# Attention, top-k and expert layer on one core: the first three head pairs get their own order of steps, PSUM banks and copy engines

## The chip, the cores and the metric

One of the eight cores of a Trainium2 chip runs the whole program. The metric is the device time of one execution in microseconds.

## The reference

Eight batches of eight heads, 576 tokens, 64 numbers a head. Attention is masked by blocks of 64 tokens: a token sees its own block and the blocks before it.

```python
scores = scale * np.matmul(q, k.transpose(0, 1, 3, 2))          # (8, 8, 576, 576)
scores = np.where(block_i >= block_j, scores, -1000000000.0)
scores = scores - np.max(scores, axis=-1, keepdims=True)
attn = np.exp(scores)
attn = attn / (np.sum(attn, axis=-1, keepdims=True) + 1e-09)
x = np.matmul(attn, v)                                          # then (8, 576, 512)
# for each batch b
scores = x[b] @ w_gate                                          # (576,)
top_idx = np.argpartition(-scores, 128)[:128]
xe = x[b, top_idx]
out[b] = x[b]
out[b, top_idx] += sigmoid(scores[top_idx])[:, None] * (np.maximum(xe @ w1, 0) @ w2)
```

## The kernel before

**Pairs and tiles.** Two heads form a pair, so there are 32 pairs, 0 to 31. A pair's scores are cut into nine tiles, t = 0 to 8: tile t is the 64 tokens of block t against the 64 (t + 1) tokens that they see, with one head in each half of the 128 partitions. So tile t is 128 x 64 (t + 1), and a shape names its tile: 320 columns are tile 4, 512 tile 7, 576 tile 8.

**The steps of a pair.** `scores(p, u)` (L374) multiplies q and k on TensorE in three parts: u = 2 writes tiles 4, 3, 0 and 2, u = 1 tiles 6, 5 and 1, u = 0 tiles 8 and 7. `maxima(p, t)` (L383) reduces a tile out of PSUM on VectorE. `exps(p, t)` (L393) takes the exponential out of PSUM into `p_sb` on ScalarE, with the maximum as bias. `turn_p(p, w)` (L438) transposes blocks of `p_sb` on TensorE into PSUM, for tile pairs (8, 7), (6, 5), (2, 1), (4, 3) and the halves "h": 16, 12, 4, 8 and 6 transposes, 46 in all. `keep_p` copies them to SBUF, on ScalarE (L217) or VectorE (L224). `times_h` (L488) and `times_v` (L500) multiply with V. `invert` and `divide` (L511, L512, L519) normalise on VectorE, and SP stores the result. `shrink` (L321) scales q on POOL (on VectorE for pair 0, L319).

**The order.** The engines work off their instructions in the order in which the program issues them, and a table sets that order: `STEPS` gives each step a time within a pair, pair p's step is due at p plus that time, and the steps of all pairs are sorted by it. The loop takes the first step that is `ready`: its inputs are issued, the pair before has issued the same step, and the PSUM banks that the step opens are free. `OVER` can give the first pairs times of their own; before, it is empty.

**PSUM.** It has eight banks of 512 columns. `BANK` names the banks of each use: ("s", g) for the score tiles, in five groups (`SETS`: 6 and 8, 7, 4 and 0, 5 and 1, 3 and 2), ("t", u) for the three groups of turns, "y" for the products with V. Odd pairs use them with 2, 3 and 4, 5 exchanged (`OTHER`). So pair 0's turns of group 1 need banks 0 and 1, which hold pair 1's tiles 5, 1 and 7 once pair 1's scores are issued.

**Fillers.** `WAKES` puts matmuls without a use (L743, 512 columns) into waits: eight at time 0.25 and six at 1.3, behind the ten at the very start.

**The rest.** Each pair's output is stored, each batch's gate scores go through ranks and indices (VectorE, POOL, `select`), and behind the attention the selected rows go through w1 and w2 (L953, L977).

Of the kernel before, what the change touches and what calls it, by code (L numbers as in the profile page):

```python
# [103 lines left out]
STORE, FETCH = 0.7, 1.4  # L104
PRELOAD = {"load": 3, "load_v": 2}
WARM, SOON, NQK, FILLS, EARLIEST, BEGIN = 10, 1, 3, 1, 4, 0.3
OVER = {}
FIRST_CUTS = ((0, 320), (320, 576))
FIRST_WRITES = {2: [(2, 0), (4, 2), (2, 4), (4, 3)]}
ENGINE_FIRST = {}  # L110
WAKES = ((0.25, 8), (1.3, 6))
HELD = (6, 7)
WIDE, SHORT, TAGS = (1, 2, 3, 0), (4, 5), {(0, 3): 'w'}
LAST_RANK, LAST_VEC, LAST_FAR = 0.2, 9, 9
# [40 lines left out]
def attention_topk_ffn(  # L155
# [75 lines left out]
    def attention(att):  # L231
# [6 lines left out]
        st = [dict() for _ in range(N)]  # L238
# [4 lines left out]

        def bank(p, use):

            return tuple(OTHER[x] for x in BANK[use]) if p % 2 else BANK[use]

        def take(p, use, reads):

            x = bank(p, use)  # L250
            for z, y in enumerate(x):
                assert live[y] is None, (p, use, live)
                live[y] = [p, use, reads[z] if isinstance(reads, list) else reads]
            return ps_all[:, x[0]:x[-1] + 1:max(x[-1] - x[0], 1), :]

        def give(p, use, part=None):
            for x in bank(p, use)[slice(None) if part is None else slice(part, part + 1)]:
                assert live[x][0:2] == [p, use], (p, use, live)
                live[x][2] -= 1
                if not live[x][2]:  # L260
                    live[x] = None

        now = [0.0]
        uses = {
            "scores": lambda u: [("s", g) for g, _ in WRITES[u]],
            "turn_p": lambda w: [("t", TURNS[w][0])], "times_h": lambda: ["y"],
            "rank": lambda: ["rk"],
        }
        takes, seen = [[] for _ in range(8)], set()
        for at, name, *args in STEPS:  # L270
            for use in uses.get(name, lambda *x: [])(*args):
                if use not in seen:
                    seen.add(use)
                    for p in range(2):
                        for x in bank(p, use):
                            takes[x].append(at + p)

        def room(x):
# [137 lines left out]
        def engine(p, *key):  # L416

            return ENGINE_FIRST.get((p, *key)) or ENGINE[key if len(key) > 1 else key[0]]

# [266 lines left out]
        def tick(kind, p):  # L686
# [15 lines left out]
            turn_p=turn_p, keep_p=keep_p, times_v=times_v, divide=divide,  # L702
# [28 lines left out]
        for p in range(N + 5):  # L731
            for i, (at, name, *args) in enumerate(STEPS):
                if name in TICKS:
                    plan += [(at + x, i, x, name, args) for x in (range(9) if not p else (p + 8,))]
                elif name not in PRELOAD or p >= PRELOAD[name]:
                    plan.append((p + (OVER.get(p, OVER.get(p - N, {})) if p < N else {}).get((name, *args), at), i, p, name, args))
        plan += [(at, -1, 0, "wake", (n,)) for at, n in WAKES]
        plan.sort()
# [23 lines left out]
        firsts = {}  # L762
# [4 lines left out]
        def ready(p, name, args):  # L767

            if p and (p - 1, name, *args) not in made and not (name in PRELOAD and p <= PRELOAD[name]):
                return False  # L770
            for other, back in needs.get(name, ()):
                if p >= back and any((p - back, other, *x) not in made for x in by_name[other]):
                    return False
            return all(
                live[x] is None
                for use in uses.get(name, lambda *x: [])(*args) if firsts[use] == (name, args) for x in bank(p, use)
            )

        parts, owner, filled, warmed = {}, {}, {}, []
# [37 lines left out]
        while (N - 1, "divide") not in made:  # L817
            blocked = set()
            for n, (at, i, p, name, args) in enumerate(plan):
                if name in TICKS or name == "wake" or p >= N or (p not in blocked and ready(p, name, args)):  # L820
                    break
                blocked.add(p)
            at, i, p, name, args = plan.pop(n)
            now[0] = at
            if name == "wake":
                wake(*args)
                continue
            if name in TICKS:
                if name == "rank" and at > N + LAST_RANK or name == "vec" and at > N + LAST_VEC or name == "far" and at > N + LAST_FAR:
                    continue  # L830
                if name != "rank" or all(live[x] is None for x in bank(p, "rk")):
                    tick(name, p)
                continue
            if p < N:
                steps[name](p, *args)
                made.add((p, name, *args))
                if name == "times_v" and p == N - 1 and fill and not warm and "last" not in parts and not any(parts[x] for x in warmed):
                    parts["last"] = list(hidden_parts(0, fill.pop(0), spare(True)))
            elif early:
                stand_in(p, name, args)  # L840
            if name == "scores" and args[0] == 1 and 2 <= p < N:
                weights(p)
            if not early and all((N - 1, "scores", u) in made for u in range(len(WRITES))):
                begin_early()
# [239 lines left out]
    with ExitStack() as att:  # L1084
        const_att = att.enter_context(tc.tile_pool(name="const_att", bufs=1))
        attention(att)
# [31 lines left out]
```

## Time and profile before

| | us |
|---|---|
| median of 3 runs | 350.02 (347.95 to 350.79) |
| profiled execution | 349.31 |
| its span, first to last instruction | 347.6 |
| TensorE matmuls busy | 333.6 (96%) |
| VectorE busy | 254.1 (73%) |
| ScalarE busy | 237.1 (68%) |
| POOL busy | 169.7 (49%) |

Busy times are those of the profiled execution; its time lies 1.7 us above its span, for what comes before the first and after the last instruction. The attention takes about the first 250 us of the span, the expert phase the rest. The shares are means over both.

### The profile page before, as it was taken

What the parts mean: (1) busy time and instruction counts of PE and PEld (TensorE: products, weight loads), DVE (VectorE), ACT (ScalarE), POOL (GpSimd) and SP (SyncE); (2) the same over time, 40 slices, a digit from 0 to 9 for tenths busy, and PEclk for the clock granted to TensorE, in tenths of its full rate; (3) what the DMA queues carried; (4) which work ended last, traced back from release to release, by engine and by line L of the source; (5) the groups of instructions that cost most, each with busy time, mean ns of one, the idle gap of its engine ahead of it and who ended that gap; (6) DMA issues with size and microseconds to landing.
All of it is one profiled execution on the core that took longest, in us unless ns stands there. A gap on an engine that the chain in (4) does not pass through costs nothing.

```text
span 347.6 us, 15612 instructions
## 1 busy us (share of the span) xinstructions
PE 333.6 (96%) x6681; PEld 278.0 (80%) x6681; DVE 254.1 (73%) x638; ACT 237.1 (68%) x554; POOL 169.7 (49%) x240
## 2 busy tenths in 40 slices
PE   8799999999999999999899999999999979999993
PEld 3488888888888888888688888889877768888882
DVE  4567789789979988988798998898296965222330
ACT  3899999999999899998889899997133101122000
POOL 2200056029980569967175895739539933210121
PEclk9999999999999999999999999999999989999998
DMA  7656677676888678666756767341230102200001
GB/s 263 215 165 197 194 214 256 202 240 175 267 245 259 205 224 248 189 182 169 196 153 214 226 177 204 101 111 36 55 84 1 38 31 62 91 31 2 30 30 60
DMA packets 42069, 52.51 MB, mean 151 GB/s; under 512 B 8680, under 2 KB 30736, under 8 KB 42000
## 3 DMA queue, kind: packets, MB, share of 16 engines
q1 hardware_dynamic: 40432, 47.03, 45.7%
q0 software_dynamic: 1280, 4.20, 3.5%
q8 instruction: 52, 0.85, 1.0%
q10 hardware_dynamic: 288, 0.30, 0.3%
q14 instruction: 17, 0.14, 0.1%
HBM read 39.94 MB, written 11.55 MB: 148 GB/s over the span
## 4 chain that ended last, share of the span: by engine, by line
PE 83%; POOL 5%; DVE 4%; issue 2%; ACT 2%; DMA 2%; POOLq 0%; DVEq 0%
PE ps L374 23%; PE ps L500 22%; PE ps L438 14%; PE ps L977 9%; PE ps L953 8%; PE ps L488 4%; POOL more L615 3%; ACT p_sb L393 2%; PE ps L924 1%; PE ps L743 1%; DMA xe<-out_dram,idx_all 1%; POOL count L615 1%; DVE junk L545 1%; DMA out_dram<-y,idx_all 1%; DVE nmax L383 1%
## 5 line engine op out<-in xcount | busy, mean ns | idle before, releaser
L393 ACT ACTIVATE p_sb<-ps,nmax 128x320 f32<-128x320 f32 (+8 forms) x288 | 130.2, 531 | 14.2 <-DVE nmax L383 7.9
L383 DVE TENSOR_REDUCE nmax<-ps 128x1 f32<-128x320 f32 (+8 forms) x288 | 118.9, 480 | 12.1 <-PE ps L374 11.7
L374 PE MATMUL ps<-qk 64*64 64x64 f32 (+6 forms) x1408 | 87.1, 386 | 2.7 <-issue 2.3
L217 ACT COPY pt<-ps 128x512 f32<-128x512 f32 (+1 forms) x192 | 82.2, 507 | 7.6 <-PE ps L438 6.0
L500 PE MATMUL ps<-v,pt 128*64 128x65 f32 x2560 | 81.3, 222 | 0.0
L500 PEld LDWEIGHTS ps<-v,pt 128*64 128x64 f32 x2560 | 77.9, 137 | 1.9
L374 PEld LDWEIGHTS ps<-qk 64*64 64x64 f32 x1408 | 48.8, 133 | 15.8 <-issue 8.8
L615 POOL TENSOR_SCALAR more<-sB,sc 64x64 int8<-64x64 f32 (+6 forms) x49 | 56.8, 1166 | 6.0 <-DMA xe<-out_dram,idx_all 3.7
L438 PE MATMUL ps<-ident,p_sb 64*128 64x64 f32 x1472 | 54.3, 225 | 2.2 <-ACT p_sb L393 2.2
L438 PEld LDWEIGHTS ps<-ident,p_sb 64*128 64x128 f32 x1472 | 49.3, 139 | 5.7 <-issue 2.0
L977 PE MATMUL ps<-w,h 128*128 128x512 f32 x192 | 47.3, 404 | 0.0
L977 PEld LDWEIGHTS ps<-w,h 128*128 128x128 f32 x192 | 36.8, 194 | 8.3
L953 PE MATMUL ps<-xeTh,w 128*128 128x512 f32 x128 | 41.6, 401 | 0.0
L959 ACT ACTIVATE h<-ps 128x512 fp32r<-128x512 f32 x16 | 9.6, 599 | 38.7 <-PE ps L953 38.7
L332 POOL MEMSET v<- 128x14 f32 x32 | 4.0, 124 | 57.0 <-DMA v<-in_vz_dram 49.2
L488 PEld LDWEIGHTS ps<-v,ph 64*64 64x64 f32 x768 | 22.3, 133 | 11.8 <-issue 11.1
L545 DVE CUSTOM_DVE_ANT_0 junk<-x_sb,wg_b 128x512 bf16<-128x512 f32 x40 | 30.8, 769 | 0.1
L987 POOL DMA_INDIRECT out_dram<-y,idx_all x8 | 8.4, 1051 | 44.9 <-DVE y L982 34.7
L960 DVE SCALAR_TENSOR_TENSOR h<-ps,h 128x512 fp32r<-128x512 f32 x16 | 11.0, 690 | 25.3 <-ACT h L959 25.3
L953 PEld LDWEIGHTS ps<-xeTh,w 128*128 128x128 f32 x128 | 24.1, 188 | 6.0
L519 DVE TENSOR_TENSOR x_sb<-ps,rinv 128x640 f32<-128x640 f32 x32 | 26.4, 825 | 1.3
L321 POOL TENSOR_SCALAR qk<-qk 128x576 f32<-128x576 f32 x31 | 22.2, 716 | 10.3 <-DMA qk<-in_qk_dram 7.7
(56 smaller groups left out, 276.2 us busy)
## 6 DMA issues: line engine op xcount, KB each, us to landing
qk<-in_qk_dram SPq DMA_DIRECT2D x31, 576.0 KB, 5.4
v<-in_v_dram SPq DMA_DIRECT2D x32, 264.0 KB, 5.2
w_raw<-in_w_dram SPq DMA_DIRECT2D x16, 256.0 KB, 2.9
out_dram<-x_sb SPq DMA_DIRECT2D x32, 128.0 KB, 3.8
out_dram<-x_sb SPq DMA_DIRECT2D x64, 64.0 KB, 3.2
v<-in_vz_dram SPq DMA_DIRECT2D x32, 99.0 KB, 4.2
sB<-line SPq DMA_DIRECT2D x8, 192.0 KB, 2.9
out_dram<-x_sb SPq DMA_DIRECT2D x32, 32.0 KB, 3.0
```

What stands on the lines that cost most here:

```text
L217: nc.scalar.copy(out=o, in_=i)
L374: nc.tensor.matmul(place(p, t)[64 * o:64 * o + 64, c0:c1], qT[:, 64 * t:64 * t + 64], kT[:, k0:k0 + c1 - c0], start=True, stop=True,)
L383: nc.vector.tensor_reduce(out=s["nmax"][:, c:c + 1], in_=place(p, t), axis=AX.X, op=ALU.max, negate=True)
L393: nc.scalar.activation(out=st[p]["p"][:, first(t):first(t) + ends(t)], in_=place(p, t), func=AF.Exp, bias=st[p]["nmax"][:, c:c + 1], scale ...
L438: nc.tensor.transpose(out=ps[:, a, at], in_=win, identity=ident[r, r])
L488: nc.tensor.matmul(y[64 * c:64 * c + 64, k:k + D + 1], s["ph"][r, a, w], block, start=(z, c) not in begun, stop=False)
L500: nc.tensor.matmul(y[64 * c:64 * c + 64, k:k + D + 1], s["pt"][:, at:at + 64], vt[:, n, hh, 0:D + 1], start=False, stop=hh == 1 and (i, n) ...
L519: nc.vector.tensor_tensor(out=x[:, :, h * D:(h + 2) * D].rearrange("p i (h d) -> p i h d", h=2), in0=outcome(p)[:, :, :, 0:D], in1=rinvs[p ...
L545: nc.vector.tensor_tensor_reduce(out=junk[:, 0:DM], in0=x[:, PLACES.index(t), :], in1=wg_b, scale=1.0, scalar=0.0, op0=ALU.mult, op1=ALU.a ...
L615: eng.tensor_scalar(out=o[r, c:c1], in0=row["sB"][r, c:c1], scalar1=sc[r, t:t + 1], scalar2=None, op0=op)
L953: nc.tensor.matmul(ps[:, 0:ncol], w1_hl[f][:, a, c, :], xeT[g][d][:, c, 0:ncol], start=(c == 0 and t == 0), stop=(c == NC1 - 1 and t == 2),)
L977: nc.tensor.matmul(ps[0:n, 0:DM], h_tile(f)[:, a, begin[g][gi]:begin[g][gi] + n], late["w2"][f][:, d, :], start=(f == 0 and t == 0), stop= ...
```

## The change

The tables for pairs 0, 1 and 2 get entries: `OVER` (times), `BANK_FIRST` (banks), `ENGINE_FIRST` (copy engines). `WAKES` keeps three matmuls of fourteen. `bank` looks into `BANK_FIRST` first. `takes`, by which a spare bank is chosen, asks for pairs 4 and 5, which have no entries. `ready` asks for the banks of each use that the pair has not opened yet, where it asked only at the step that opens a use first in the common table.

```diff
-OVER = {}
+OVER = {
+    0: {
+        ('scores', 2): -0.5767,
+        ('scores', 0): -0.477,
...
+    1: {
+        ('scores', 2): -0.5402,
...
-ENGINE_FIRST = {}
-WAKES = ((0.25, 8), (1.3, 6))
+ENGINE_FIRST = {
+    (0, 'keep_p', (2, 1)): 'act',
+    (0, 'keep_p', (4, 3), 0): 'dve',
+    (0, 'keep_p', (6, 5), 0): 'dve',
+    (0, 'keep_p', (6, 5), 1): 'dve',
+    (0, 'keep_p', (8, 7), 1): 'dve',
+    (1, 'keep_p', (2, 1)): 'act',
+    (1, 'keep_p', (4, 3), 1): 'dve',
+    (1, 'keep_p', (8, 7), 1): 'dve',
+    (2, 'keep_p', (4, 3), 1): 'dve',
+    (2, 'keep_p', (6, 5), 0): 'dve',
+    (2, 'keep_p', (8, 7), 0): 'dve',
+    (2, 'keep_p', (8, 7), 1): 'dve',
+}
+BANK_FIRST = {
+    (0, ('s', 0)): (3, 4),
+    (0, ('s', 1)): (0,),
+    (0, ('s', 2)): (1,),
...
+    (0, ('t', 0)): (1, 4),
+    (1, ('s', 1)): (3,),
...
+}
+WAKES = ((0.25, 3),)
...
         def bank(p, use):
 
+            if (p, use) in BANK_FIRST:
+                return BANK_FIRST[p, use]
             return tuple(OTHER[x] for x in BANK[use]) if p % 2 else BANK[use]
...
-                        for x in bank(p, use):
+                        for x in bank(p + 4, use):
...
-                for use in uses.get(name, lambda *x: [])(*args) if firsts[use] == (name, args) for x in bank(p, use)
+                for use in uses.get(name, lambda *x: [])(*args) if use not in st[p] for x in bank(p, use)
```

The lines of the new kernel are 136 to 138 higher: L374 becomes L512, L438 L576, L383 L521, L393 L531, L217 L353, L224 L360, L743 L881, L488 L626, L500 L638.

TensorE, before, from the first turns of pair 0 on (qk1 is pair 1's q and k, p_sb_150 holds pair 0's exponentials; the fillers between are left out):

```order
L438 MATMUL ps_93<-ident_71,p_sb_150 128x64 x16
L374 MATMUL ps_93<-qk1_121 64x64 x2
L374 MATMUL ps_93<-qk1_121 64x256 x4
L374 MATMUL ps_93<-qk1_121 64x192 x2
L374 MATMUL ps_93<-qk1_121 64x64 x2
L374 MATMUL ps_93<-qk1_121 64x448 x2
L374 MATMUL ps_93<-qk1_121 64x384 x2
L374 MATMUL ps_93<-qk1_121 64x128 x2
L374 MATMUL ps_93<-qk1_121 64x64 x2
L374 MATMUL ps_93<-qk1_121 64x512 x4
```

and TensorE after, at the same place:

```order
L512 MATMUL ps_93<-qk1_121 64x64 x2
L512 MATMUL ps_93<-qk1_121 64x256 x4
L512 MATMUL ps_93<-qk1_121 64x192 x2
L512 MATMUL ps_93<-qk1_121 64x64 x2
L576 MATMUL ps_93<-ident_71,p_sb_150 128x64 x16
L512 MATMUL ps_93<-qk1_121 64x448 x2
L512 MATMUL ps_93<-qk1_121 64x384 x2
L512 MATMUL ps_93<-qk1_121 64x128 x2
L512 MATMUL ps_93<-qk1_121 64x64 x2
L512 MATMUL ps_93<-qk1_121 64x512 x4
L576 MATMUL ps_93<-ident_71,p_sb_150 128x64 x16
```

Part 2 of pair 1's scores has moved ahead of pair 0's turns (8, 7), and the turns (2, 1) and (6, 5) of pair 0 follow pair 1's scores directly, where six fillers stood. Pair 2's scores are cut in the same way, around the turns "h" and (4, 3) of pair 0 and (8, 7) of pair 1.

ScalarE, before, the first eleven exponentials and copies between (pt takes the turned blocks):

```order
L393 ACTIVATE p_sb<-ps,nmax 128x320
L393 ACTIVATE p_sb<-ps,nmax 128x64
L393 ACTIVATE p_sb<-ps,nmax 128x384
L393 ACTIVATE p_sb<-ps,nmax 128x128
L393 ACTIVATE p_sb<-ps,nmax 128x256
L393 ACTIVATE p_sb<-ps,nmax 128x512
L393 ACTIVATE p_sb<-ps,nmax 128x576
L393 ACTIVATE p_sb<-ps,nmax 128x448
L393 ACTIVATE p_sb<-ps,nmax 128x192
L217 COPY pt<-ps 128x2x4x64 x2
L393 ACTIVATE p_sb<-ps,nmax 128x320
L393 ACTIVATE p_sb<-ps,nmax 128x64
```

and after:

```order
L531 ACTIVATE p_sb<-ps,nmax 128x256
L531 ACTIVATE p_sb<-ps,nmax 128x512
L531 ACTIVATE p_sb<-ps,nmax 128x64
L531 ACTIVATE p_sb<-ps,nmax 128x320
L531 ACTIVATE p_sb<-ps,nmax 128x128
L531 ACTIVATE p_sb<-ps,nmax 128x576
L531 ACTIVATE p_sb<-ps,nmax 128x384
L531 ACTIVATE p_sb<-ps,nmax 128x448
L353 COPY pt<-ps 128x2x4x64
L531 ACTIVATE p_sb<-ps,nmax 128x192
L531 ACTIVATE p_sb<-ps,nmax 128x256
L531 ACTIVATE p_sb<-ps,nmax 128x192
```

Tile 7 (512 columns) is now second, and one of the two copies of the turns (8, 7) has gone to VectorE. The next rows there are pair 1's tiles 0, 4 and 5, the copy of (2, 1), and tiles 7, 1, 8 and 6.

VectorE, before, from the end of pair 0's scaling to the first normalising step:

```order
L319 TENSOR_SCALAR qk_120<-qk_120 128x256
L383 TENSOR_REDUCE nmax<-ps 128x1 x18
L224 COPY pt<-ps 128x2x128
L383 TENSOR_REDUCE nmax<-ps 128x1 x9
L511 TENSOR_SCALAR rinv_115<-ps 128x10
```

and after:

```order
L457 TENSOR_SCALAR qk_120<-qk_120 128x256
L521 TENSOR_REDUCE nmax<-ps 128x1 x13
L360 COPY pt<-ps 128x2x4x64
L521 TENSOR_REDUCE nmax<-ps 128x1 x5
L360 COPY pt<-ps 128x2x3x64 x2
L360 COPY pt<-ps 128x2x2x64
L521 TENSOR_REDUCE nmax<-ps 128x1
L360 COPY pt<-ps 128x2x4x64
L521 TENSOR_REDUCE nmax<-ps 128x1 x8
L649 TENSOR_SCALAR rinv_115<-ps 128x10
```

Five copies, two of 512 columns, two of 384 and one of 256, stand among the maxima of pairs 1 and 2, where one of 256 stood.

## Rows read from the trace of the kernel before

**Rows 1.** Chain that ended last, in order of time: start us, us, what.

```profile
7.47 3.01 ACT p_sb L393 x6
10.61 0.72 PE ps L438 x16
...
14.05 3.00 ACT p_sb L393 x6
...
17.09 1.16 PE ps L438 x30
18.25 2.59 PE ps L374 x34
20.84 0.40 PE ps L488 x21
21.23 2.48 PE ps L500 x80
23.72 1.59 PE ps L438 x46
...
28.30 2.48 PE ps L500 x80
...
170.58 1.68 issue
...
257.58 1.22 POOL xe L910
```

**Rows 2.** Timeline of VectorE, ScalarE and POOL at the start (a line begins with start and length).

```profile
5.65 3.78 DVE L383 TENSOR_REDUCE nmax<-ps 128x1 f32<-128x320 f32 x9 [0.79 <-PE ps L374]
7.10 0.28 DVE L383 TENSOR_REDUCE nmax<-ps 128x1 f32<-128x128 f32 x1
12.33 3.67 DVE L383 TENSOR_REDUCE nmax<-ps 128x1 f32<-128x320 f32 x9 [2.89 <-PE ps L374]
...
6.37 0.73 ACT L393 ACTIVATE p_sb<-ps,nmax 128x320 f32<-128x320 f32 x2 [3.17 <-DVE nmax L383]
7.47 3.31 ACT L393 ACTIVATE p_sb<-ps,nmax 128x384 f32<-128x384 f32 x7 [0.36 <-PE ps L374]
17.23 2.12 ACT L217 COPY pt<-ps 128x384 f32<-128x384 f32 x5
19.56 0.45 ACT L217 COPY pt<-ps 128x256 f32<-128x256 f32 x1
...
8.26 0.67 POOL L321 TENSOR_SCALAR qk<-qk 128x576 f32<-128x576 f32 x1 [6.20 <-DMA qk<-in_qk_dram]
```

**Rows 3.** Groups of the attention phase by shape: count, busy us, mean ns, idle before.

```profile
L393 ACT ACTIVATE p_sb<-ps,nmax 128x576 f32<-128x576 f32 x32 | 23.7, 742 | 0.0
L393 ACT ACTIVATE p_sb<-ps,nmax 128x64 f32<-128x64 f32 x32 | 10.4, 326 | 0.0
L217 ACT COPY pt<-ps 128x512 f32<-128x512 f32 x64 | 39.3, 615 | 0.6 <-PE ps L438 0.6
L217 ACT COPY pt<-ps 128x256 f32<-128x256 f32 x62 | 26.1, 420 | 0.0
L383 DVE TENSOR_REDUCE nmax<-ps 128x1 f32<-128x576 f32 x32 | 23.9, 746 | 0.0
L383 DVE TENSOR_REDUCE nmax<-ps 128x1 f32<-128x256 f32 x32 | 13.2, 413 | 0.0
L224 DVE COPY pt<-ps 128x256 f32<-128x256 f32 x31 | 13.1, 423 | 7.9 <-ACT pt L217 7.8
L519 DVE TENSOR_TENSOR x_sb<-ps,rinv 128x640 f32<-128x640 f32 x30 | 24.7, 825 | 1.2
```

**Rows 4.** Busy time by stretch: from:to, length, engines' busy (instructions), clock, DMA share, GB/s.

```profile
7.40:10.80 3.40, 2.05 (x16) 0.88 (x16) 2.03 (x4) 3.31 (x7) 0.80 (x2) 1.00 1.03 357
...
277.00:280.30 3.30, 0.62 (x4) 0.19 (x3) 3.22 (x5) 0.00 (x0) 3.14 (x5) 1.00 0.25 79
280.30:283.70 3.40, 3.40 (x11) 2.82 (x12) 2.15 (x6) 0.68 (x2) 0.67 (x3) 0.51 0.00 0
```

More of the change, by code (lines that the diff above doesn't have):

```diff
@@ L106 @@
 WARM, SOON, NQK, FILLS, EARLIEST, BEGIN = 10, 1, 3, 1, 4, 0.3
-OVER = {}
+OVER = {
+    0: {
+        ('scores', 2): -0.5767,
+        ('scores', 0): -0.477,
+        ('maxima', 3): -0.302,
+        ('exps', 3): -0.1788,
+        ('maxima', 4): -0.141,
+        ('scores', 1): -0.0966,
+        ('maxima', 0): -0.0466,
+        ('maxima', 7): 0.0297,
+        ('exps', 7): 0.1077,
+        ('exps', 0): 0.1109,
+        ('maxima', 8): 0.1557,
+        ('maxima', 1): 0.2044,
+        ('exps', 1): 0.2684,
+        ('maxima', 6): 0.3275,
+        ('exps', 8): 0.4103,
+        ('maxima', 5): 0.5343,
+        ('exps', 5): 0.5391,
+        ('maxima', 2): 0.6182,
+        ('exps', 6): 0.6411,
+        ('turn_p', (8, 7)): 0.724,
+        ('keep_p', (8, 7), 0): 0.8353,
+        ('exps', 2): 1.1684,
+        ('keep_p', (8, 7), 1): 1.352,
+        ('turn_p', (2, 1)): 1.5231,
+        ('turn_p', (6, 5)): 1.5774,
+        ('keep_p', (2, 1)): 1.6571,
+        ('keep_p', (6, 5), 0): 1.6954,
+        ('turn_p', 'h'): 1.7251,
+        ('keep_p', (6, 5), 1): 1.7506,
+        ('turn_p', (4, 3)): 1.7668,
+        ('keep_p', (4, 3), 0): 1.8394,
+        ('keep_p', 'h'): 2.0243,
+        ('times_h',): 2.2006,
+        ('times_v',): 2.6673,
+    },
+    1: {
+        ('scores', 2): -0.5402,
+        ('maxima', 3): -0.2796,
+        ('maxima', 2): -0.2761,
+        ('scores', 1): -0.193,
+        ('exps', 3): -0.0245,
+        ('exps', 2): 0.1627,
+        ('maxima', 0): 0.193,
+        ('maxima', 4): 0.2928,
+        ('maxima', 5): 0.3606,
+        ('maxima', 1): 0.3751,
+        ('exps', 4): 0.4392,
+        ('maxima', 7): 0.4756,
+        ('maxima', 6): 0.5438,
+        ('exps', 5): 0.5938,
+        ('exps', 7): 0.7075,
+        ('exps', 1): 0.7528,
+        ('exps', 8): 0.7667,
+        ('turn_p', (8, 7)): 0.7853,
+        ('keep_p', (8, 7), 0): 0.9566,
+        ('keep_p', (8, 7), 1): 0.9711,
+        ('turn_p', (2, 1)): 1.027,
+        ('turn_p', (6, 5)): 1.2343,
+        ('turn_p', 'h'): 1.3647,
+        ('keep_p', (6, 5), 0): 1.8815,
+        ('keep_p', (4, 3), 1): 1.9278,
+        ('keep_p', (2, 1)): 2.0073,
+        ('keep_p', (6, 5), 1): 2.0118,
+        ('keep_p', 'h'): 2.0436,
+        ('keep_p', (4, 3), 0): 2.0895,
+        ('times_h',): 2.1132,
+        ('times_v',): 2.3763,
+        ('invert',): 2.7787,
+    },
+    2: {
+        ('scores', 2): -0.2493,
+        ('maxima', 0): -0.1389,
+        ('scores', 1): -0.0871,
+        ('maxima', 4): -0.0279,
+        ('scores', 0): 0.0198,
+        ('maxima', 3): 0.1995,
+        ('exps', 4): 0.253,
+        ('exps', 5): 0.296,
+        ('maxima', 6): 0.3957,
+        ('maxima', 1): 0.4711,
+        ('maxima', 7): 0.4772,
+        ('exps', 6): 0.5281,
+        ('maxima', 8): 0.5521,
+        ('exps', 7): 0.7361,
+        ('maxima', 2): 0.7536,
+        ('exps', 8): 0.8447,
+        ('turn_p', (8, 7)): 0.8904,
+        ('keep_p', (8, 7), 0): 0.9003,
+        ('exps', 3): 0.9081,
+        ('keep_p', (8, 7), 1): 0.9784,
+        ('turn_p', (2, 1)): 1.1483,
+        ('turn_p', (6, 5)): 1.4614,
+        ('turn_p', 'h'): 1.6316,
+        ('keep_p', (6, 5), 0): 1.6598,
+        ('keep_p', (2, 1)): 1.739,
+        ('turn_p', (4, 3)): 1.7705,
+        ('keep_p', (4, 3), 1): 1.8286,
+        ('keep_p', (6, 5), 1): 1.9424,
+        ('keep_p', (4, 3), 0): 2.0905,
+        ('times_h',): 2.2698,
+        ('times_v',): 2.5678,
+        ('invert',): 2.8718,
+        ('divide',): 2.8871,
+    },
+}
@@ L112 @@
+BANK_FIRST = {
+    (0, ('s', 0)): (3, 4),
+    (0, ('s', 1)): (0,),
+    (0, ('s', 2)): (1,),
+    (0, ('s', 3)): (2,),
+    (0, ('s', 4)): (7,),
+    (0, ('t', 0)): (1, 4),
+    (1, ('s', 1)): (3,),
+    (1, ('s', 2)): (5,),
+    (1, ('s', 3)): (2,),
+    (1, ('s', 4)): (0,),
+    (1, ('t', 0)): (0, 7),
+    (2, ('s', 1)): (0,),
+    (2, ('s', 2)): (5,),
+    (2, ('s', 3)): (1,),
+    (2, ('s', 4)): (4,),
+}
+WAKES = ((0.25, 3),)
 HELD = (6, 7)
```

## The prediction

> **What bounds the kernel now.** I read the chain of waits in order of time first [rows 1]. From 17.09 us on it runs on TensorE without a break: turns, scores, the two groups of products with V, turns again. Two ends of the big group of products (L500), 21.23 + 2.48 = 23.71 and 28.30 + 2.48 = 30.78, are 7.07 us apart, so a pair costs 7.07 us of TensorE. Before 17.09 the chain twice leaves TensorE for ScalarE, for 3.01 us at 7.47 and for 3.00 us at 14.05: TensorE has scored a pair and has nothing to do until that pair's exponentials are out. The timeline of ScalarE and VectorE [rows 2] says why ScalarE is late: its exponentials of pair 0 begin at 6.37, but the bulk of pair 1's only at 14.05 [rows 1], since pair 1's scores stood behind pair 0's first turn (10.61), which itself waited for pair 0's exponentials. The engines take turns instead of overlapping. In steady state ScalarE is nearly full too: nine exponentials take 0.73 + 3.31 = 4.04 us and seven copies 19.56 + 0.45 - 17.23 = 2.78, in all 6.8 of 7.07. So only the start has something to give, and everything behind it moves as a block if TensorE gets there earlier.
>
> **Prices.** By the groups of instructions [rows 3] an exponential costs 326 ns at 64 columns and 742 at 576, on a line of 0.81 ns a column; a maximum 413 ns at 256 and 746 at 576, 1.04 ns a column. In a row each begins before the last has ended: seven exponentials of 3.95 us in all fill 3.31 [rows 2], so 0.106 is taken off for each follower; nine maxima of 4.32 us fill 3.67, so 0.08 off; ScalarE's seven copies (615 ns at 512 columns, 420 at 256, two, three and two of 512, 384 and 256) of about 3.6 us fill 2.78, so 0.13 off. Handing over: a first maximum at 5.65 of 320 columns and one of 64 end at 6.26, ScalarE begins at 6.37, about 0.10. ScalarE's 14.05 + 3.00 = 17.05 to TensorE's 17.09 [rows 1] is 0.04.
>
> **The new start, step by step.** SP's and POOL's instructions keep their order, and so do all engines' from pair 3 on; the edits to the two tests (`takes`, `ready`) choose at build time and issue nothing. TensorE's scores of pair 1 now wait only for POOL's scaling of qk, 8.26 + 0.67 = 8.93 [rows 2], not for the first turn; they are cut around that turn. The chain that I find goes through ScalarE, in its new order of tiles:
> VectorE starts at 5.65 as before. Maxima 3, 4 and 0 (256, 320 and 64 columns) end the stretch at 6.52, maximum 7 (512) at 7.20. ScalarE's second instruction is now exponential 7, so it waits until 7.30, 0.7 us longer than its work needs, with exponentials 0 and 4 ready behind it: this order is worse there. Exponentials 7, 0 and 4 take 1.23, to 8.53; tile 1's (128) ends at 8.91. Maximum 5 waits for that one, whose bank it shares, with maximum 2 and all of pair 1's behind it; it starts at 9.01 and ends at 9.56. ScalarE takes tiles 5 and 6 from 9.66 to 10.67, one copy of 512 columns (615 - 130 ns) to 11.16, tile 2 of pair 0 and tiles 3, 2, 0, 4, 5 of pair 1 (2.15) to 13.31, the copy of (2,1) (0.29) to 13.60, tiles 7 and 1 (0.86) to 14.46, and tile 8 (0.74) ends at 15.20. TensorE's turns (8,7) of pair 1 start at 15.24. Before, that was 17.09.
> From there TensorE has no wait on my list: 16 of 46 turns (1.59 x 16 / 46 = 0.55), scores 1 and 0 of pair 2 (2048 of 2880 columns of 2.59 us, 1.84), 0.40 and 2.48 [rows 1]. The products of pair 0 end at 20.51 instead of 23.71: 3.2 us earlier.
> Some of it is given back at once. VectorE has five copies in this start instead of one: between maximum 8 of pair 1 and the first wide maximum of pair 2 stand copies of 384, 384, 256 and 512 columns, so ScalarE begins pair 2's exponentials at about 17.4; 4.04 us of them with some 0.5 of waits end at 21.9, and TensorE, which arrives at the turns that need the last of them at 20.51 + 1.11 = 21.62, waits 0.3. One pair later I count 0.1 to 0.2 again. I take 0.5: **2.7 us gained.** After that the order is that of before, and the period is TensorE's 7.07 again.
>
> **Costs that no row shows.** VectorE never copied 512 or 384 columns out of PSUM. Its copy of 256 columns takes 423 ns where the maximum of 256 takes 413 [rows 3], so I take the maxima's line: 0.69 and 0.56. Below, a copy of 512 costs at least the 423 ns of 256; above, at most the 825 ns of the 640-column multiplication from PSUM. The low end would take 0.26 off each, and spare up to 0.3 us in the sum; the high end adds 0.14 to each of four copies, 0.6 off the gain. The eleven dropped filler matmuls (14 become 3, at about 0.22 us) filled only waits, so I cost them at nothing; the cover is that TensorE has real work in the same stretch (see the clock below). Pair 1's scores now depend on a landing at 8.26: the turn behind them has 0.3 us to spare before ScalarE misses its copy, and beyond that each microsecond of delay costs one.
>
> A rule of the Trainium skill belongs to the step of maximum 5. The row shows it: exponential 5 of pair 0 begins at 7.47, 0.09 after the maximum of tile 1, which shares its bank, has ended (7.10 + 0.28 = 7.38), though its own maximum was done when that one began, about 7.18 [rows 2]. "PSUM — Partial Sum Buffer", section "PSUM bank collisions raise a hardware error", says that two engines must not touch one bank at once, two reads included, so a program has to keep them apart by bank. The trace agrees. By it the new order pays 0.4 us on VectorE for putting tile 1's exponential ahead of maximum 5, and ScalarE 0.2; without it the sum would be 2.9.
>
> **To the end.** The last long piece of the chain starts from VectorE's indices and POOL's gather at 257.58 [rows 1]; both come from data of this same attention phase, so they move with it. The profiled execution took 349.31 us (span 347.6); 2.7 off is 346.6. Against the median of the runs shown, 350.02, it is **347.3 us**, and that is my number.
>
> **Rivals.**
> A, the forecast: 2 to 3.4 us gained, 347.3. Chance 0.60.
> B, most of the gain is given back, 349.0. ScalarE has 0.25 us to spare in a pair, so what VectorE's new copies make late stays late; if each of seven copies costs 0.25 more than on the line, 1.7 is lost. One more wait of TensorE like that at 170.58 ("issue", 1.68 us [rows 1]), at another place because the stream is 22 instructions shorter, would cost the same. For it: VectorE's copies are unmeasured. Against: the copy of 256 lies on the line. 0.18.
> C, slower. TensorE's clock falls in the patchy start, since fillers are gone. It shows in this trace when TensorE was busy 0.62 of 3.30 us: the next stretch had 0.51 of the clock, the level of 1.2 GHz [rows 4]. Where it was busy 2.05 of 3.40 us (7.40 to 10.80) it kept 1.00, or 2.4 GHz. In the new order I count there three fillers 0.65, scores 0.75, sixteen turns 0.72 and 0.4 of the next scores, 2.5, more than before; and 2.7 and 2.9 in the two stretches up to 17.60. If the clock were at half in both of these all the same, 5.6 us of work would need 11.2 where 6.8 are: 4.4 lost, 351.7. With one stretch low 2.0 is lost and 0.7 still gained, so it decides from the second on. 0.05.
> D, more: ScalarE never waits. Its work up to the last copy for pair 0 is 18 exponentials (8.08) and five copies (1.9), from 6.2 to 16.2; then 0.40 and 2.48 end at 19.1, 4.6 gained and 0.4 given back: 345.8. For it: the waits at 6.6 and 9.5 hang on how soon scores reach VectorE, which I know only from another order. Against: TensorE's 15.24 rests on tile 8's exponential alone. 0.17.
>
> **How the numbers follow.** The runs shown reach from 347.95 to 350.79, so about 1% is what a measurement of this kernel can tell from no change. A is 0.8% off the median. Faster by over 1% (under 346.5) is D's 0.17 and 0.05 of A: 0.22. Slower by over 1% (over 353.5) needs more than C, or a mishap that I don't see: 0.03. Within 1%: 0.75. The range of 345.3 to 349.9 takes in A with the bounds of the copies, B and D, and half a microsecond of noise on the side of the gain.
>
> **What would show it.** In the profile after: the exponentials of pair 1 without a break of over 0.3 us from about 11.2 to 15.7; turns (8,7) of pair 1 at 15.2; the first L638 group (the old L500) ending near 20.5 and the third 7.07 us after the second; ScalarE's first wait of about 0.7 us after one exponential; copies of 512 columns on VectorE at 0.69 us; the clock at 1.00 up to the late expert phase. A first L638 end after 22.5, a period over 7.1 us in pairs 2 to 5, or a clock under 1.00 before 20 us would prove the steps wrong.

## The result, and the profile after

| | us |
|---|---|
| after, median of 4 runs | 347.11 (345.32 to 348.19) |
| before, beside it, median of 4 runs | 350.40 (347.95 to 351.45) |
| ratio after to before, 95% interval | 0.990 (0.985 to 0.995) |
| predicted | 347.3 (345.3 to 349.9) |
| profiled execution after, its span | 348.19, 346.5 |

The ratios here and below leave out runs over 1.5% above the fastest of their kernel, while the medians hold every run. The time came out as forecast. The two profiled executions differ by only 1.1 us (349.31 and 348.19), less than the forecast of 2.7, so the start has to be read piece by piece. The chain of waits of the kernel after, in order of time (start us, us, what), answers to [rows 1]:

```profile
4.72 0.85 PE ps L881 x2
5.57 1.53 PE ps L512 x18
...
7.13 1.56 DVE nmax L521 x4
...
8.71 2.30 ACT p_sb L531 x5
...
11.05 0.71 PE ps L576 x15
11.77 2.17 PE ps L512 x20
...
14.62 0.37 ACT pt L353
14.99 0.86 ACT p_sb L531 x2
...
15.89 1.35 PE ps L576 x30
17.24 1.93 PE ps L512 x18
19.17 0.35 PE ps L626 x24
19.52 2.48 PE ps L638 x80
...
26.57 2.48 PE ps L638 x80
...
33.67 2.49 PE ps L638 x80
...
51.85 0.41 issue
```

Two things are to be seen. First, ScalarE's two long holds on the chain, 3.01 and 3.00 us before, are now 2.30 and 0.37 + 0.86: the first part of pair 1's scores (9.48, in the timeline below) stands ahead of pair 0's first turns and no longer waits for them, and five of pair 1's exponentials (in the row at 12.36) run beside the scores and turns from 11.77 to 14.60. Second, VectorE's first maximum begins at 7.13 where it began at 5.65. Nothing in the change stands ahead of it. The chain begins with the last of the ten first fillers: in this execution the clock went to its full level (1.00, 2.4 GHz) at 6.75 us (before: 3.86), so they ended at 5.57 instead of 4.79 and pair 0's scores ran partly at half clock (1.2 GHz). The same kernel run once more (run 1 below) had the rise at 3.78 and its first maximum at 5.71. In nine further profiles below, all with ten first fillers, the rise came anywhere from 3.8 to 7.1 us. So from here on I count from VectorE's first maximum, which takes out this chance of one execution: pair 0's products with V end at 19.52 + 2.48 = 22.00, **14.87 us** behind it. Before that was 23.71 - 5.65 = 18.06; the forecast was 20.51 - 5.65 = 14.86. The next ends are 29.05 and 36.16, periods of 7.05 and 7.11.

The timeline of ScalarE, VectorE and TensorE answers to [rows 2] (start and length first):

```profile
7.59 0.47 ACT L531 ACTIVATE p_sb<-ps,nmax 128x256 f32<-128x256 f32 x1 [4.38 <-DVE nmax L521]
8.71 3.29 ACT L531 ACTIVATE p_sb<-ps,nmax 128x512 f32<-128x512 f32 x7 [0.65 <-DVE nmax L521]
11.90 0.59 ACT L353 COPY pt<-ps 128x512 f32<-128x512 f32 x1
12.36 2.21 ACT L531 ACTIVATE p_sb<-ps,nmax 128x192 f32<-128x192 f32 x6
14.62 0.37 ACT L353 COPY pt<-ps 128x256 f32<-128x256 f32 x1
14.89 2.11 ACT L531 ACTIVATE p_sb<-ps,nmax 128x512 f32<-128x512 f32 x4
17.22 0.86 ACT L353 COPY pt<-ps 128x512 f32<-128x512 f32 x2 [0.23 <-PE ps L576]
...
18.53 0.53 ACT L531 ACTIVATE p_sb<-ps,nmax 128x320 f32<-128x320 f32 x1
19.26 3.62 ACT L531 ACTIVATE p_sb<-ps,nmax 128x384 f32<-128x384 f32 x8 [0.21 <-DVE nmax L521]
...
7.13 5.13 DVE L521 TENSOR_REDUCE nmax<-ps 128x1 f32<-128x256 f32 x13 [2.29 <-PE ps L512]
...
12.91 2.75 DVE L521 TENSOR_REDUCE nmax<-ps 128x1 f32<-128x384 f32 x5
15.57 1.50 DVE L360 COPY pt<-ps 128x384 f32<-128x384 f32 x3
...
9.48 0.99 PE L512 MATMUL ps<-qk 64*64 64x64 f32 x20
```

ScalarE waits 0.65 after one exponential and then runs from 8.71 to 17.00 with no gap in brackets; before, it stood still between its two blocks. VectorE's thirteen maxima of two pairs run in one block. The groups of VectorE's copies by shape, over the attention phase, answer to [rows 3]:

```profile
L360 DVE COPY pt<-ps 128x256 f32<-128x256 f32 x33 | 13.9, 422 | 5.6 <-ACT pt L353 5.2
L360 DVE COPY pt<-ps 128x512 f32<-128x512 f32 x4 | 2.7, 686 | 0.1
L360 DVE COPY pt<-ps 128x384 f32<-128x384 f32 x3 | 1.6, 546 | 0.0
```

And the busy times by stretch, as in [rows 4] (the last three numbers of a row are granted clock, DMA share and GB/s):

```profile
10.16:13.58 3.42, 3.04 (x50) 1.71 (x42) 3.28 (x10) 3.42 (x10) 0.79 (x2) 1.00 0.79 252
13.58:16.99 3.41, 3.01 (x69) 2.35 (x66) 3.24 (x8) 3.36 (x8) 0.67 (x1) 1.00 0.57 192
279.80:283.20 3.40, 3.40 (x10) 2.62 (x9) 2.38 (x6) 0.68 (x2) 0.09 (x1) 0.50 0.00 0
```

TensorE is busy 3.0 of 3.4 us where it had been busy 2.05, the clock stays at 1.00 up to the same late stretch in the expert phase, and that stretch is as low as before.

### The profile page after: what moved, and what is told of

Read it like the earlier page. It is cut to its first block, busy times and chain, and to the rows that moved or that the text cites. A ratio compares the mean times of both kernels' runs of the same rounds, so it can differ in the third digit from the quotient of the medians.

```text
span 346.5 us, 15593 instructions
## 1 busy us (share of the span) xinstructions
PE 334.8 (97%) x6670; PEld 278.9 (81%) x6670; DVE 258.7 (75%) x646; ACT 233.5 (67%) x546; POOL 169.2 (49%) x240
## 4 chain that ended last, share of the span: by engine, by line
PE 86%; POOL 5%; issue 2%; DVE 2%; DMA 2%; ACT 1%; POOLq 0%
PE ps L512 24%; PE ps L638 23%; PE ps L576 15%; PE ps L1115 9%; PE ps L1091 8%; PE ps L626 4%; POOL more L753 3%; PE ps L881 1%; DMA xe<-out_dram,idx_all 1%; PE ps L1062 1%; ACT p_sb L531 1%; POOL count L753 1%; DMA out_dram<-y,idx_all 1%; PE ps L764 1%; POOL count L755 1%
## 5 line engine op out<-in xcount | busy, mean ns | idle before, releaser
L531 ACT ACTIVATE p_sb<-ps,nmax 128x192 f32<-128x192 f32 (+8 forms) x288 | 129.9, 532 | 15.2 <-DVE nmax L521 8.1
L521 DVE TENSOR_REDUCE nmax<-ps 128x1 f32<-128x256 f32 (+8 forms) x288 | 119.2, 479 | 8.5 <-PE ps L512 8.0
L512 PE MATMUL ps<-qk 64*64 64x64 f32 (+6 forms) x1408 | 89.4, 389 | 1.5 <-issue 1.4
L353 ACT COPY pt<-ps 128x384 f32<-128x384 f32 (+2 forms) x184 | 78.9, 506 | 8.6 <-PE ps L576 7.2
L638 PE MATMUL ps<-v,pt 128*64 128x65 f32 x2560 | 82.2, 223 | 0.3
L638 PEld LDWEIGHTS ps<-v,pt 128*64 128x64 f32 x2560 | 78.5, 138 | 2.4 <-issue 0.5
L512 PEld LDWEIGHTS ps<-qk 64*64 64x64 f32 x1408 | 50.1, 135 | 16.5 <-issue 9.9
L576 PE MATMUL ps<-ident,p_sb 64*128 64x64 f32 x1472 | 54.1, 225 | 0.8 <-ACT p_sb L531 0.8
L576 PEld LDWEIGHTS ps<-ident,p_sb 64*128 64x128 f32 x1472 | 49.1, 139 | 4.5 <-ACT p_sb L531 2.1
L626 PEld LDWEIGHTS ps<-v,ph 64*64 64x64 f32 x768 | 22.6, 133 | 12.0 <-issue 10.4
L683 DVE CUSTOM_DVE_ANT_0 junk<-x_sb,wg_b 128x512 bf16<-128x512 f32 x40 | 31.5, 787 | 0.1
L1080 ACT ACTIVATE gate<-gate 128x1 f32<-128x1 f32 x8 | 1.6, 203 | 37.5 <-DVE gate L1076 37.5
```

Of the source, the lines that this page charges most:

```text
L353: nc.scalar.copy(out=o, in_=i)
L512: nc.tensor.matmul(place(p, t)[64 * o:64 * o + 64, c0:c1], qT[:, 64 * t:64 * t + 64], kT[:, k0:k0 + c1 - c0], start=True, stop=True,)
L521: nc.vector.tensor_reduce(out=s["nmax"][:, c:c + 1], in_=place(p, t), axis=AX.X, op=ALU.max, negate=True)
L531: nc.scalar.activation(out=st[p]["p"][:, first(t):first(t) + ends(t)], in_=place(p, t), func=AF.Exp, bias=st[p]["nmax"][:, c:c + 1], scale ...
L576: nc.tensor.transpose(out=ps[:, a, at], in_=win, identity=ident[r, r])
L626: nc.tensor.matmul(y[64 * c:64 * c + 64, k:k + D + 1], s["ph"][r, a, w], block, start=(z, c) not in begun, stop=False)
```

## The experiments

Eleven runs. Line numbers move with some edits, so each run says what its lines are where they are not those of the kernel after. Beside the ratio, each is read by one number of its profile: the time from VectorE's first maximum to the end of pair 0's second group of products, with the ends of the next three pairs behind it. The kernel before has 18.07, 25.13, 32.17, 39.23 there, the kernel after 14.87, 21.93, 29.03, 36.10 (from single instructions). So the change gains 3.2, 3.2, 3.1 and 3.1 us.

**1. The kernel after once more**, without an edit.

> The changed kernel once more, as the mark for the other runs of this set. Both theories: 0.990 of the kernel before, about 347.1 us. The stretch from VectorE's first maximum to the end of pair 0's large group of products with V was 18.06 us in the kernel before (5.65 to 23.71) and 14.87 after (7.13 to 22.00). It should be 14.9 again, wherever the first maximum falls. If the first maximum moves between 5.6 and 7.2 us from run to run with the time at which TensorE's clock rises, the later start of the profiled execution was chance and no part of the change.

Median 348.26 (347.06 to 349.70, 10 runs), before 352.71 (348.97 to 357.50, 33 runs), ratio 0.991 (0.987 to 0.994). Ends at 15.10, 22.16, 29.25, 36.60, with the clock's rise at 3.78 and the first maximum at 5.71. This execution shows what takes over where the first scores are early. Its chain:

```profile
1.74 6.45 DMA qk<-in_qk_dram
...
8.27 0.68 POOL qk L459
...
9.00 0.99 PE ps L512 x15
...
18.33 2.48 PE ps L638 x80
```

Pair 1's q and k land at 8.19, and its scores wait for POOL's scaling of them; that costs 0.2 here. The gain is confirmed, and this execution shows it without any correction for the start: its first maximum is as early as that of before (5.71 and 5.65), and pair 0's products end at 18.33 + 2.48 = 20.81 instead of 23.71, 2.9 us earlier.

**2. Fewer fillers in the old order** (before with three).

```diff
-WAKES = ((0.25, 8), (1.3, 6))
+WAKES = ((0.25, 3),)
```

> The kernel before with three filler matmuls instead of fourteen, and nothing else. Theory (the order makes the gain, the fillers filled waits): no change, 350.4 us within 0.3%, the stretch 18.0 to 18.1 us. Rival (TensorE's queue is freed by the missing fillers): most of the gain is here already, 347.5 us, stretch 15.5. Rival (the fillers kept the clock up): 351 to 352.5 us, with a clock under 1.00 somewhere between 8 and 20 us.

Median 354.48 (349.35 to 361.14, 13 runs) to 352.71, ratio 1.002 (0.997 to 1.007). The one profiled execution had 20.91 instead of 18.07, and in it the clock was at 0.50 from 13.54 to 16.96 and from 20.37 to 23.78. By time nothing is decided, but the cover that I had named for the fillers, the clock, turned out to be real in this execution of the old order.

**3. No filler behind the first ten, in the old order**, profiled in two executions.

```diff
-WAKES = ((0.25, 8), (1.3, 6))
+WAKES = ()
```

> The kernel before without any filler behind the first ten. Theory from the run of before with three fillers, where the stretch from the first maximum to the end of pair 0's second group of products was 20.9 us with two low stretches of the clock: the same two low stretches, 20.9 us or more, ratio 1.002 to 1.012. Rival, that clock was one execution's chance: clock 1.00 up to 25 us and a stretch of 18 us.

> A second profile of the kernel before without fillers behind the first ten. Its timed runs had a mean granted clock of 0.981 to 0.992, eight of ten under 0.990, and the one profiled was one of the two above. Theory: the low clock of the others lies in the start, between 10 and 27 us, as in the run of before with three fillers (two stretches at 0.50 there and 2.8 us more up to the end of pair 0's second group of products, 20.9 behind the first maximum). Rival: it lies elsewhere, in the expert phase, and the start has 1.00 and 18.1 us.

Timed: 354.44 (351.45 to 357.60, 10 runs) to 353.71 (349.71 to 362.73, 35 runs), ratio 1.000 (0.996 to 1.005). The first profile contradicts run 2: the clock is 1.00 in the whole start, and the ends are 18.15, 25.20, 32.25, as with fourteen fillers. The second repeats run 2: 20.86, 27.91, 34.96. Busy times in the start of the first execution:

```profile
10.49:13.90 3.41, 1.75 (x40) 1.57 (x44) 0.52 (x3) 2.86 (x6) 0.80 (x2) 1.00 0.54 202
13.90:17.32 3.42, 1.88 (x25) 0.64 (x17) 3.42 (x9) 2.52 (x8) 0.67 (x1) 1.00 0.21 63
```

and of the second execution of the same kernel:

```profile
8.60:12.06 3.46, 0.77 (x22) 0.73 (x26) 1.51 (x3) 2.91 (x8) 1.19 (x3) 1.00 0.98 304
12.06:15.48 3.42, 3.42 (x40) 2.67 (x44) 1.04 (x4) 1.76 (x4) 0.88 (x3) 0.50 0.11 40
15.48:18.89 3.41, 1.83 (x24) 0.70 (x16) 2.72 (x6) 2.65 (x6) 0.00 (x0) 1.00 0.42 120
18.89:22.30 3.41, 3.01 (x46) 2.90 (x50) 0.42 (x1) 3.10 (x8) 0.61 (x2) 0.50 0.70 239
```

The same order of work leaves the same holes, and in one execution they cost the clock and 2.7 us, in the other nothing. So in themselves the fillers cost and win nothing in the old order (18.15 to 18.07); what they win there is that the clock falls less often, though in the times (ratio 1.000) that doesn't show. The mean granted clock of every timed run says how often: under 0.990 it was in 8 of the 10 timed runs of this kernel, and in 26 of 91 runs of the kernel before (11 of the 35 beside this one). It doesn't say where: the profiled execution of the new order with fourteen fillers (run 4) had a mean of 0.988 with a full clock in its whole start, and its low stretch, from 285.71 to 292.53, lay in the expert phase.

**4. Fillers in the new order**: fourteen as before, and none.

```diff
-WAKES = ((0.25, 3),)
+WAKES = ((0.25, 8), (1.3, 6))
```

> The changed kernel with the fourteen fillers of before. Theory: the fillers now stand ahead of real work, above all six of 0.22 us between pair 1's scores and pair 0's turns; ScalarE's copy of the turns (2, 1) comes about 1 us later: stretch 15.8 us, 348.0 us, 0.9 more than the changed kernel. Rival (fillers only keep the clock): as the changed kernel, 347.1, or better.

```diff
-WAKES = ((0.25, 3),)
+WAKES = ()
```

> The kernel after without its last three fillers. From VectorE's first maximum to the end of pair 0's second group of products (the stretch that was 18.06 us before and 14.87 after): theory, the new order fills this stretch with real work, so the clock stays at 1.00 and the stretch is 14.9 us, the ratio to before 0.990. Rival, the three fillers that were kept guard the clock: a row in the first 21 us shows it near 0.5, and the stretch is 16.5 us or more, ratio 0.996 or above.

Fourteen: 352.28 (345.74 to 357.32, 13 runs) to 352.71, ratio 0.994 (0.988 to 0.999); ends 16.60, 23.66, 30.74. Its chain shows why:

```profile
8.34 1.83 PE ps L881 x8
...
13.80 1.40 PE ps L881 x6
15.20 0.66 PE ps L576 x16
...
15.89 0.37 ACT pt L353
```

The fillers (L881) are on the path: the six stand ahead of pair 0's turns, and ScalarE's copy of these turns follows behind them. Their 1.40 is most of the 1.7 lost, twice the 0.9 that I expected. None: 349.95 (348.91 to 353.08, 12 runs) to 353.71, ratio 0.993 (0.989 to 0.997), ends 14.88, 21.94, 29.04, clock 1.00 up to the end of the expert phase, and a mean clock under 0.990 in none of the 12 runs. So the new order doesn't need the three that were kept, and with all of them it loses, by the chain, about half its gain.

**5. The new order with the old copy engines.**

```diff
-ENGINE_FIRST = {
-    (0, 'keep_p', (2, 1)): 'act',
...
-}
+ENGINE_FIRST = {}
```

> The changed kernel with no entries in ENGINE_FIRST: the copies of the first three pairs go to the engines of before, so ScalarE gets back copies that VectorE had taken. Theory (the start runs at ScalarE's pace): stretch 16.5 us, and 1.4 more lost in the next pair, so the whole gain is gone, 350.1 to 350.7 us. Rival (order and banks make the gain, engines are a detail): 347.1 to 347.8 us, stretch 15.0 to 15.5.

Median 353.63 (351.42 to 355.75, 12 runs) to 352.71, ratio 1.007 (1.003 to 1.011), the only kernel here that is surely slower than before. Ends 17.00, 25.69, 33.01, 40.05. Its timeline, TensorE and ScalarE (L563 are the turns, L518 the exponentials, L340 and L347 the copies of ScalarE and VectorE):

```profile
17.30 0.71 PE L563 MATMUL ps<-ident,p_sb 64*128 64x64 f32 x15 [1.72 <-ACT p_sb L518]
18.31 0.71 PE L563 MATMUL ps<-ident,p_sb 64*128 64x64 f32 x15 [0.30 <-ACT p_sb L518]
...
15.92 0.48 ACT L340 COPY pt<-ps 128x384 f32<-128x384 f32 x1 [0.95 <-DVE pt L347]
```

The copies stand between the exponentials that TensorE waits for (1.72 and 0.30 us), one of them behind a wait of 0.95 for a copy of VectorE, and the next pair pays again (25.69 - 17.00 = 8.69 where 7.07 is the period). VectorE's copies are no side matter of the change: without them nothing of its gain is left. The chain accounts for 0.8 us of the slowdown against before (40.05 to 39.23); for the rest of the 0.7%, some 1.6 us, no cause is shown.

**6. The tables of pairs 0 and 1 alone.** The edit takes pair 2's times, engines and banks out of the three tables.

```diff
 OVER = {
...
-    2: {
-        ('scores', 2): -0.2493,
...
-    },
 }
```

> The tables of pairs 0 and 1 alone; pair 2's times, banks and engines are those of the common table. Theory, the gain is won in the first two pairs: from the first maximum pair 0's second group of products ends at 15.6 us and pair 1's at 22.7 (after: 14.87 and 21.93), so 2.3 of the 3.2 us stay and the ratio to before is 0.993. Rival, pair 2's entries carry it (its scores stand ahead of pair 0's last turns): 17 us or more, ratio 0.997 or above.

Median 350.86 (348.76 to 352.82, 12 runs) to 353.71, ratio 0.994 (0.989 to 0.998). Ends 15.59, 23.00, 30.05, 37.11: 2.5 us of the gain at pair 0's end, 2.1 from pair 1 on (22.7 was expected for the second end). In its chain the scores (L469) between the last turns and the products of pair 0 take 2.59 us (34 instructions) where after they take 1.93 (18):

```profile
17.29 2.59 PE ps L469 x34
```

Without entries pair 2's scores stand whole behind the turns. So pair 2's entries are worth 1.0 of the 3.1.

**7. The new order with the old banks.**

```diff
-BANK_FIRST = {
-    (0, ('s', 0)): (3, 4),
...
-}
+BANK_FIRST = {}
```

> The kernel after with the common table's PSUM banks for all pairs; times and engines are the new ones. Theory, the new times need the new banks, since a step whose banks are still held is put off: pair 0's second group of products ends 18.6 us after the first maximum, as late as before (18.06) or later, ratio 1.000 to 1.004. Rival, the times alone make the gain and the banks are a detail: 15.5 us or less, ratio 0.993 or below.

Median 356.08 (351.51 to 358.60, 12 runs) to 353.71, ratio 1.003 (0.997 to 1.008). Its first maximum begins at 6.52. Its timeline of TensorE (L496 are the scores, L560 the turns, L337 ScalarE's copies, L515 its exponentials):

```profile
12.84 2.71 PE L496 MATMUL ps<-qk 64*64 64x448 f32 x44 [0.67 <-ACT pt L337]
16.57 1.15 PE L560 MATMUL ps<-ident,p_sb 64*128 64x64 f32 x30 [1.01 <-ACT p_sb L515]
18.91 1.03 PE L560 MATMUL ps<-ident,p_sb 64*128 64x64 f32 x16 [1.20 <-ACT p_sb L515]
20.61 3.69 PE L496 MATMUL ps<-qk 64*64 64x448 f32 x24 [0.67 <-ACT pt L337]
```

Scores wait for copies of turned blocks (L337), since both need the same banks; the engines take turns again as before the change. The sixteen turns (8, 7) of pair 1 at 18.91 are 12.39 behind the first maximum, where after they begin 9.40 behind it. Up to there the clock was full. At 19.06 it fell, and the scores at 20.61 took 3.69 instead of 1.93: hence a part of 21.36 in the end where I expected 18.6; of the 6.5 us more than after, 3.0 were there before the clock fell. So the new times don't work without the new banks; the new banks without the times were not run.

**8. Eight first fillers instead of ten**, alone and with pair 0's exponentials 4 and 0 ahead of 7.

```diff
-WARM, SOON, NQK, FILLS, EARLIEST, BEGIN = 10, 1, 3, 1, 4, 0.3
+WARM, SOON, NQK, FILLS, EARLIEST, BEGIN = 8, 1, 3, 1, 4, 0.3
```

> The kernel after with eight filler matmuls at the very start instead of ten. Theory: in the profile of after the scores of pair 0 stood ready (VectorE's scaling ends at 4.84) and TensorE began them at 5.50, behind ten fillers at half clock that end at 5.58; with eight they end near 4.7, the scores begin at 4.9 and VectorE's first maximum at 6.5 instead of 7.13, the rest moves with it, 0.6 us or 0.2% of the time, ratio 0.987 to 0.990 where that of after is 0.990. Rival: the clock rises later for it, the first maximum is at 7.1 or later and nothing is won or some tenths are lost.

The second kernel has this besides:

```diff
-        ('exps', 0): 0.1109,
+        ('exps', 0): 0.0200,
...
+        ('exps', 4): 0.0210,
```

> As the run with eight first fillers, and pair 0's exponentials of tiles 4 and 0 stand ahead of that of tile 7. The prediction called the new order worse there, since ScalarE waits 0.7 us for tile 7's maximum with tiles 4 and 0 ready. Theory: ScalarE's early wait shrinks to under 0.3 us but the end of pair 0's second group of products stays at 14.8 to 15.0 us behind the first maximum, since maximum 5 and the exponentials behind it wait for tile 1's bank all the same. Rival: the wait is on the path, and the stretch is 14.5 us or less.

Against 352.98 (347.86 to 356.01, 23 runs) they took 349.96 (345.66 to 351.01, 12 runs) and 348.50 (346.42 to 353.28, 12 runs), ratios 0.998 (0.993 to 1.002) and 0.995 (0.991 to 1.000). Neither is shown to beat the kernel after, which was not run beside them, and the expected 0.987 to 0.990 is missed: by its ratio the first is not even shown to be faster than the kernel before, although the median of all its runs is 3.0 us lower and its chain has the whole gain at pair 0; its time is left open. The first had its clock's rise at 4.96, the first maximum at 5.81, and then ran into the landing that run 1 shows (its scores of pair 1 begin at 8.90, with 0.66 of waiting for POOL); its end is 14.90. The second had the rise at 6.93, later than after's, and its first maximum all the same at 6.47 instead of 7.13: this is the 0.6 us expected. But its scores then ran longer at half clock, and its end is 15.17. ScalarE's waits in it (L532 are the exponentials):

```profile
6.93 1.26 ACT L532 ACTIVATE p_sb<-ps,nmax 128x256 f32<-128x256 f32 x3 [3.73 <-DVE nmax L522]
8.37 0.69 ACT L532 ACTIVATE p_sb<-ps,nmax 128x512 f32<-128x512 f32 x1 [0.18 <-DVE nmax L522]
9.38 0.37 ACT L532 ACTIVATE p_sb<-ps,nmax 128x128 f32<-128x128 f32 x1 [0.32 <-DVE nmax L522]
9.91 1.74 ACT L532 ACTIVATE p_sb<-ps,nmax 128x576 f32<-128x576 f32 x3 [0.17 <-DVE nmax L522]
```

Three waits of 0.18 + 0.32 + 0.17 = 0.67 stand where one of 0.65 was, so the wait did not shrink to under 0.3 as I expected. In this execution ScalarE waits for VectorE's maxima in sum, not for tile 7's alone.

## Why the prediction was right, and where it was not

**The chain: right, step by step.** From the first maximum (5.65 in the forecast, 7.13 in the profile), by single instructions of the trace:

| step | predicted | measured |
|---|---|---|
| exponentials 7, 0, 4 of pair 0 end | 2.88 | 2.89 |
| maximum 5 begins | 3.36 | 3.19 |
| tiles 5, 6 end | 5.02 | 4.88 |
| tile 8 of pair 1 ends | 9.55 | 9.34 |
| its turns (8,7) begin | 9.59 | 9.40 |
| pair 0's products end | 14.86 | 14.87 |

The exact end is luck in part: two misses of 0.2 cancel. ScalarE was 0.2 earlier, and behind the turns TensorE took 5.47 instead of 5.27, mostly because I priced sixteen turns as a share of 46 (0.55), where a group of sixteen by itself takes 0.7, as a row that I had quoted showed [rows 1]. Run 1 shows that miss uncancelled: it starts as the forecast assumed, with the first maximum at 5.71 and POOL's scaling done at 8.95, its tile 8 ends 9.58 behind the first maximum (forecast 9.55), and its end is 15.10. The late start of the profiled execution had hidden the landing, which the forecast had counted as free.

**The bank wait: right in kind, wrong in size.** Maximum 5 did begin right behind tile 1's exponential (9.90 + 0.38 = 10.28, it begins at 10.31, and a semaphore of ScalarE is the only one that it waits for), so the rule of the Trainium skill that I drew on ("PSUM — Partial Sum Buffer", "PSUM bank collisions raise a hardware error") agrees again with the trace. But VectorE stood still for 0.08 us, not 0.4, and ScalarE, which I charged with 0.2, had no gap there. Three small things share the difference: VectorE came about 0.15 later to this maximum, because tile 8's had waited 0.06 for its scores and then took its full 0.76; tile 1's exponential ended 0.11 sooner than forecast; and the handing over took 0.03, not 0.10.

**"0.5 given back": wrong, and the largest miss of the sum.** The gain is still 3.2 at pair 1's end and 3.1 at the next two. I let pair 2's exponentials begin at 17.4, that is 11.75 behind the first maximum, and gave them 0.5 us of waits; they began at 18.53 - 7.13 = 11.40 with a single wait of 0.21, and the last one ended at 22.88. TensorE, whose products end at 22.00, comes at 22.97 to the turns whose bank this last exponential (tile 3) sets free, the last fourteen of the 46, and begins them without a gap. So it had less than 0.1 to spare where I had it wait 0.3: the step that failed is this wait, with the 0.1 to 0.2 that were to follow a pair later, and it failed narrowly.

**VectorE's copies: right.** 686 and 546 ns, for 690 and 560 on the maxima's line. They lie clearly between the two bounds (423 and 825).

**The fillers at nothing: right, with the cover right and a side overlooked.** Without them the old order takes 18.15 instead of 18.07 where the clock stays up, and TensorE's real work is what keeps it up in the new one: none of 12 runs without a filler fell under 0.990. That the new order would pay 1.7 us for keeping all fourteen the prediction had not seen: it priced the fillers by the waits that they had filled, without asking what would stand behind them in the new order.

**The rivals.** B, "mostly given back", fell with the 0.5. C, the falling clock, has the danger on the wrong side: it is the old order that is patchy. In the first batch 23 of the 33 runs of before had a mean clock of 0.990 or more and a median of 351.33, 3.07 above the 348.26 of the kernel after, close to the 3.1 of the trace; in the second, the same difference (24 of 35 runs of before) to the kernel after without fillers is 352.83 - 349.95 = 2.88. The ten others of the first batch had 355.61, and none of the ten runs of after was like them. So the distance of all runs, 352.71 - 348.26 = 4.45, is the shorter chain and a little more, which goes with these ten. Where the clock fell in them is not shown, since none of them was profiled; the old order with fewer fillers shows it in the start, the new order with fourteen in the expert phase. D, "ScalarE never waits", fell with the 0.65 before tile 7.

**The time.** 347.3 was forecast and 347.11 measured. The 3.2 of pair 0's end off the profiled 349.31 would give 346.1. What brings the profiled execution of after to 348.19 is the late rise of the clock (1.48 at the first maximum) and 0.6 more from pair 0's end to pair 31's (225.2 us for 224.5), as waits of TensorE ("issue" in the chain after) come and go at other pairs in every execution; in the profile of run 4 without fillers the same stretch took 230.4, at full clock. One of these waits, the 0.41 at 51.85, makes the period from pair 4 to pair 5 7.53, which the forecast had named as a sign that its steps are wrong (over 7.1 us in pairs 2 to 5). No step of the start explains it, and the kernel before has the like elsewhere (1.68 at 170.58 [rows 1]), so the sign was too sharp; what sets these waits off is not shown. At this kernel's spread a median of four runs cannot tell 346.8 from 347.3, so the time alone does not show the missing 0.5; the chain does.

## What to carry to other kernels

Where the chain of waits shows two engines taking turns in the start of a pipeline, put the next item's independent work ahead of the wait, and check that buffers and the engines for the copies follow: here the times without the banks or without the copy engines were no faster than the old order. Count such a gain from the first event behind the warm-up to the same end in each pair, since whole executions differ by more than it, and look also at an execution that starts as early as the old one: a late start hid the wait for pair 1's q and k here. And when real work moves into a hole that fillers guarded, take the fillers out with it: they were free while the hole was there, and 1.4 us of the path after.

## What was not expected of the hardware

The clock's rise from half (1.2 GHz) to full (2.4 GHz) came at 3.78 to 7.08 us into the span in the runs above, behind the same ten fillers, and with it the first maximum lay between 5.65 and 7.16. The same holes in TensorE's work cost the clock in one execution and not in another (run 3): TensorE was busy 0.77 and 1.83 us ahead of the two low stretches, and 1.75 and 1.88 ahead of stretches that stayed at full clock. What decides between them the profile doesn't show. And the second transfer of q and k let POOL begin between 6.1 and 8.6 us in these runs, which makes it the next bound of the start: in run 1, where it began at 8.27, pair 1's scores already waited 0.86 us for it.
